# Fill matmuls, measured arrivals in the planner, and four low parts moved from GpSimd to VectorE in a fused attention, expert and MLP kernel

## The chip, the core and the metric

The kernel runs on one core of a Trainium2 chip. The metric is the device time of one execution in microseconds (us). Engines are named as the profile names them: PE is TensorE (matmuls; PEld is its weight load), DVE is VectorE, ACT is ScalarE, POOL is GpSimd, SP is SyncE, which issues most of the transfers.

## What is computed

Three stages follow each other, all in float32.

Attention: q, k, v of shape (4, 8, 576, 64); scores are q.k/8 plus a slope per head times the distance, kept for the 128 latest keys alone, then a softmax and the product with v. The result is 2304 rows of 512 numbers, x.

Experts: each row is normalised, multiplied by eight normalised expert vectors and divided by tau; the best expert is taken, and its softmax probability is the row's weight. The row of the output is `gate * (relu(x @ w1[e]) @ w2[e])`, with w1 of (8, 512, 1024) and w2 of (8, 1024, 512).

MLP: `h = x @ w_in` (512 to 2048), then 0 below -1, h above 1 and (h+1)^2/4 between, then `@ w_out`.

## The kernel before

Products of float32 accuracy are made from two parts of each operand: a high part, which is the operand rounded by a ScalarE copy (`whi`, `kh`, `hh`), and a low part, which is the operand less its high part (`wlo`, `kl`, `hl`), a subtraction on VectorE or GpSimd.

**Attention** is cut into 72 units: 8 groups `g` (a pair of batches and a pair of heads) by 9 tiles `t` of 128 queries. Tiles 0 to 3 take the first batch of the pair, 4 to 7 the second, and tile 8 the last 64 queries of both. A unit (`unit`, L802 on) goes through these steps: scores on PE (`sc`, L826 and L827; L822 for tile 8), mask and maximum on DVE (`ss`, `mx`, L839), exponential on ACT (`at`, L847), transposes on PE (`tp`, L854), their copy on DVE or ACT (`aT`, L859, L861), the product with the values on PE (`av`, L873), and in `finish` the division by the row sums (`rs`, L884, L886). Beside it run: the loads of q and k (`qk_loads`, 16 of them, the first in two cuts of columns, L608; then L621), their split into parts (`split_block`, L659 to L665; `split_rest`, L675 and L677, for tile 8), small products of the values with the expert vectors (`ven_steps`, `ep`, L690), and the routing of the rows.

**Routing** runs for the first half of the rows (pair 0) within attention, and for the second half at its end. `route` picks each row's expert and its slot, with a count on PE (`rp`, L361 to L365) and masks (`ocp`, `oap`) that PE turns into tables (`tabp`, L404). `roots(pr)` takes the root of the rows' squares in small steps over 128x9 numbers (`root`, L117 to L141), on POOL for pair 0 and on DVE for pair 1. `gates(pr)` makes the weights (L476 to L506) and a table of them (`tabg`, L519).

**Between attention and the expert loop** PE takes 128 rows of the first expert through that expert early and unsplit (`first_rows`: `hpe`, L1172; `hTe`, L1185; `ye`, L1197), while DVE ends the routing. The rest of the rows are gathered by POOL (L1119), scaled, transposed (`bx`) and split (`xh`, `xl`). In this time four chunks of the first expert's weights are split for the loop: `conv` asks for a high part on ACT (L536) and a low part on POOL (L541). After its low part, `convert_lo` issues the load of chunk i+6 on SP.

**The expert loop** (L1363 on) and the MLP follow, with PE busy nearly all the time.

**The order of the work** up to the expert loop comes from a planner that runs when the kernel is built. Every piece of work is a stream that yields an `ask`: an engine with a planned cost, an earliest time, events to wait for, a ring of buffers. `drive` picks the ask that can start first (ties by rank), issues its instruction and moves on, so each engine's order of instructions is the planned one; the chip then executes each engine's list in that order. An ask with `port=True` is planned so that DVE and POOL don't run such steps at the same time (`held`). `arrival` plans when a load lands. `warm_up` issues nine bf16 matmuls of 512 columns, and more until planned time 10.5, as long as nothing else is to be done on PE. The planned end of attention is `base`, and CONV gives for each of the four chunks the earliest high part and low part after it.

Of the kernel before, what the change touches and what calls it, by code (L numbers as in the profile page):

```python
# [8 lines left out]
F32 = mybir.dt.float32  # L9
# [10 lines left out]
P = 128  # L20
B, H, S, D = 4, 8, 576, 64
# [7 lines left out]
NP = B // 2  # L29
# [3 lines left out]
NRAW, NW, LEAD = 6, 7, 5  # L33
NEARLY = 5
BIAS = {"V": 1.2}
CONV = ((0, 0.0, 1.0), (1, 0.9, 1.5), (2, 3.0, 9.0), (3, 4.5, 11.0))
PEN = (0.03, 0.0, 0.8)
NWARM = 9
WARM = 10.5
TICK = 3.4133  # L40
EROOT = "V"
LATE = (0.4, 0.2, 0.5, 0.5, 0.2, 0.3)
# [9 lines left out]
C1 = D + 1 + E  # L52
# [7 lines left out]
def fused_kernel(ctx, tc, qk, vT, v, emb, tau, w1, w2, win64, wout64, out):  # L60
# [94 lines left out]
    streams, asks, rank_of = [], {}, {}  # L155
    busy = dict.fromkeys("PAVGS", 0.0)
    seen, rings, work, held = {}, {}, {}, {}
    now, end, on, at_unit = [0.0], [0.0], ["", None], [0.0]

    def ask(engines, start=0.0, after=(), ring=None, late=None, duty=None, port=False):  # L160

        return engines, start, after, ring, late, duty, port

    def add(stream, rank=0.0, ready=None):
        rank_of[stream] = rank
        asks[stream] = None, now[0] if ready is None else ready, (), None, 0.0, None, False
        streams.append(stream)
# [20 lines left out]
    def drive(more):  # L188
        while more():
            best = None  # L190
            for s in streams:
                c = first_start(s)
                if c and (best is None or c[:2] < best[0][:2]):
                    best = c, s
            (_, _, e, took, start), s = best
            ring = asks[s][3]
            if ring:
                rings[ring].remove(min(rings[ring]))
            if e == "P":

                k = int(start / TICK)
                work[k] = work.get(k, 0.0) + took * (asks[s][5] or 1.0)
                if work.get(k - 1, 0.0) < 0.375 * TICK:
                    took *= 2
            now[0], end[0], on[:] = max(now[0], start), start + took, [e, s]
            if e:
                busy[e] = end[0]
                if asks[s][6]:
                    held[e] = end[0]
            r = next(s, StopIteration)  # L210
            if r is StopIteration:
                streams.remove(s)
            elif r is None:
                asks[s] = vec()
            elif isinstance(r, tuple):
                asks[s] = r
            else:
                asks[s] = None, start + r, (), None, None, None, False
# [5 lines left out]
    dma = [0.0]  # L224

    def arrival(size):
        dma[0] = max(dma[0], end[0] + 0.65) + size / 0.36e6
        return dma[0] + 0.9

    rs_ = ExitStack()  # L230
    pr_ = rs_.enter_context(tc.tile_pool(name="pr", bufs=1, side="right"))
# [224 lines left out]
    def roots(pr):  # L456

        cols = slice(pr * NT, (pr + 1) * NT)
        yield ask({"V": 0.08}, after=of_tiles("squares", pr * NT, NT) + of_tiles("most squares", pr * NT, NT))
        nc.vector.tensor_tensor(nsq[:, cols], nsq[:, cols], nsq3[:, cols], op=ALU.add)  # L460
        e = "V" if pr == NP - 1 else "G"
        yield from root_steps(pr_, nrm[:, cols], nsq[:, cols], "p", e)
        seen["root", pr] = end[0] + 0.13

    def root_steps(pool_, out_, s_, nm, e):
        for n, _ in enumerate(root(pool_, out_, s_, nm, nc.vector if e == "V" else nc.gpsimd)):
            yield ask({"V": 0.08} if n < 2 or e == "V" else {"G": 0.19}, end[0] + 0.13, port=True)
# [94 lines left out]
    with ExitStack() as a:  # L562
# [38 lines left out]
        def qk_loads(n):  # L601
            g, b = divmod(n, 2)
            if n == 0:
                raw[0, 0] = new_raw()
                for c, cols in enumerate(CUT):
                    for x in range(2):
                        yield ask({"S": 0.45})
                        nc.sync.dma_start(raw[0, 0][:, x, :, cols], qk[0, 0, :, x, :, cols])  # L608
                        seen["qk"[x], 0, 0, c] = seen["qk"[x], 0, 1, c] = arrival(P * 8 * (cols.stop - cols.start))
                    if c == 0:  # L610
                        yield ask({"S": 0.45})
                        nc.sync.dma_start(embt, emb)
                        seen["emb"] = arrival(0)
            else:
                yield ask({"S": 0.45}, after=[("loads", n - 1)] + ([("split", n - 3)] if n >= 3 else []))
                raw[g, b] = new_raw()
                pr, hp = divmod(g, H // 2)
                for x in range(2):
                    if x:
                        yield ask({"S": 0.45})  # L620
                    nc.sync.dma_start(raw[g, b][:, x], qk[2 * pr + b, hp, :, x])  # L621
                    seen["qk"[x], n] = arrival(P * 8 * S)
            seen["loads", n] = now[0]
# [75 lines left out]

        CUT = (slice(0, 256), slice(256, S))  # L700
        lpt = pa.tile([P, NT, H, E], F32, name="lpt")

        def raw_experts():

# [57 lines left out]
        def warm_up():  # L762

            t = pa.tile([P, 1], BF16, name="warm")
            nc.vector.memset(t, 0.0)
            w = ps_av.tile([P, 512], F32, tag="av", name="warm_up")
            again = lambda: nc.tensor.matmul(w, t.to_broadcast([P, P]), t.to_broadcast([P, 512]), start=True, stop=True)
            for i in range(NWARM):
                again()
            busy["P"] = 0.87 + 0.427 * NWARM  # L770
            work.update({0: 0.5 * (TICK - 0.87), 1: 0.5 * (busy["P"] - TICK)})
            while True:
                yield ask({"P": 0.215}, late=LATE[5])
                if now[0] > WARM:
                    break
                again()
            rings["av"].append(end[0])

        def bias_of(h):
            yield ask({"V": 0.35}, 2.1)  # L780
# [21 lines left out]
        def unit(i):  # L802
# [61 lines left out]
            yield ask({"P": 0.449 * nb}, end[0] + 0.15, order("s3") + [("ven", g, x) for x in ((0, 1) if b is None else (b,))], None if n else "av", duty=0.57)  # L864
            seen["s3", u] = end[0]
            if n == 0:
                av_t[g] = ps_av.tile([P, 2, 2, C1], F32, tag="av", name="av")
            av = av_t[g]
            for j in range(2):
                for x, o in ((b, slice(0, P)),) if b is not None else ((0, slice(0, D)), (1, slice(D, P))):  # L870
# [60 lines left out]
            nc.gpsimd.memset(t, 0.0)  # L931
        nc.gpsimd.memset(one, 1.0)
        busy.update(A=0.7, V=0.5, P=0.5, S=0.63, G=3.0)
        rings.update(xp=[0.0] * 2, sc=[0.0] * 2, ss=[0.0] * 2, at=[0.0] * 4, tp=[0.0] * 2, aT=[0.0] * 3, av=[0.0])
        add(warm_up(), 1000.0)
        def load_tau():
            yield ask({"S": 0.45}, 5.0)
            nc.sync.dma_start(taut, tau.rearrange("(a b) -> a b", a=1).broadcast_to([E, 1]))
# [26 lines left out]
            add(gates(pr), rank + 5.0)  # L965
        add(early_rows(), 61.0)
        drive(lambda: len(finished) < len(units))


    pool = lambda st, name, bufs, **k: st.enter_context(tc.tile_pool(name=name, bufs=bufs, reuse_waits="tile", **k))  # L970
# [119 lines left out]
    with ExitStack() as bb:  # L1090
# [60 lines left out]
        def conv(i, t, j, u):  # L1151

            yield ask({"A": 0.95}, base + t, [("raw", i)])
            convert_hi(i, pw)
            yield ask({"G": 2.31}, max(end[0] + 0.13, base + u), [("lo", j - 1)] if j else [])
            convert_lo(i, nc.gpsimd, i + NRAW < 8)
            seen["lo", j] = end[0]
            if i + NRAW < 8:
                raws[i + NRAW] = wraw[i + NRAW]
                seen["raw", i + NRAW] = arrival(P * 4096)  # L1160
# [447 lines left out]
```

## Time and profile before

| | |
|---|---|
| median of 3 runs | 841.91 us (841.09 to 844.17) |
| the profiled execution | 842.7 us, span 841.0 us |
| busy share of the span | PE 97%, PEld 90%, DVE 63%, ACT 50%, POOL 17% |
| mean granted clock of PE | 0.979 of full speed |
| attention ends, first matmul of the expert loop | about 180 us, 204.01 us |

In the rows below, a timeline row has the start in us, the duration in us, engine, line, operation, output and input names with shapes and a count, and in brackets the idle time before it with what ended it. A row of the stretches has its limits, its length, and the busy time of PE, PEld, DVE, ACT and POOL with the instruction count of each; then the granted clock of PE (1.00 is 2.4 GHz, 0.50 is 1.2 GHz), the share of the DMA engines, and GB/s.

### The profile page before, as it was taken

Reading aid. Unit: us, or ns where it says so; the run is one execution under the profiler, and the core shown is the slowest. Engines: PE = TensorE matmul, PEld = TensorE weight load, DVE = VectorE, ACT = ScalarE, POOL = GpSimd, SP = SyncE. Lnnn points to the kernel's source line nnn. Section 1 sums busy time; section 2 is a strip of 40 time slices with the busy share of each in tenths; the row PEclk is TensorE's granted clock in tenths of the full one; section 3 lists DMA queues with packets and bytes.
Section 4 is the critical chain, followed back from the end, with each engine's and each line's share of the span. In section 5 each row is a group of like instructions: output and inputs, shape, how many; then the busy total and the mean of one; then the engine's idle time right before and its main releaser. Section 6 shows DMA issues by size and latency. Waiting matters only on the chain.

```text
span 841.0 us, 14144 instructions
## 1 busy us (share of the span) xinstructions
PE 816.4 (97%) x5195; PEld 757.7 (90%) x5195; DVE 529.9 (63%) x1390; ACT 419.4 (50%) x871; POOL 145.8 (17%) x206
## 2 busy tenths in 40 slices
PE   7999999879999999999999999999999999999996
PEld 5999898767999999999999989898999999999995
DVE  6676787599667767877639998644334445334332
ACT  5769888673553465667525555433222234223222
POOL 3756754226101001100000000003000003001001
PEclk7899999898999999999999999999999999999999
DMA  8566866035754486778323443022000012000000
GB/s 317 192 212 232 316 221 231 15 125 158 244 184 160 141 282 220 244 250 270 113 63 113 137 123 129 1 76 76 1 1 0 1 37 77 1 1 38 1 1 37
DMA packets 59690, 106.00 MB, mean 126 GB/s; under 512 B 3942, under 2 KB 36710, under 8 KB 59616
## 3 DMA queue, kind: packets, MB, share of 16 engines
q1 hardware_dynamic: 56288, 95.15, 34.4%
q0 software_dynamic: 3328, 9.90, 3.3%
q8 instruction: 41, 0.67, 0.3%
q14 instruction: 33, 0.27, 0.1%
HBM read 90.42 MB, written 14.62 MB: 125 GB/s over the span
## 4 chain that ended last, share of the span: by engine, by line
issue 55%; PE 11%; POOL 2%; DVE 1%; ACT 1%; DMA 0%; POOLq 0%; ACTq 0%
POOL out L1537 2%; PE bh L1411 2%; PE bh L1413 2%; PE bh L1412 2%; PE by L1400 2%; PE by L1402 2%; PE by L1401 2%; PE bx L1248 1%; DMA wraw<-in_w 0%; ACT whi L536 0%; DVE wlo L541 0%; POOL gap L1536 0%; POOL xg L1119 0%; PE permp L1338 0%; ACT yo L1450 0%
## 5 line engine op out<-in xcount | busy, mean ns | idle before, releaser
L1492 PE MATMUL ch<-yh,wc_0h 128*128 128x384 f32 x384 | 129.2, 336 | 0.0
L1494 PE MATMUL ch<-yh,wc_0l 128*128 128x384 f32 x384 | 129.1, 336 | 0.0
L1493 PE MATMUL ch<-yl,wc_0h 128*128 128x384 f32 x384 | 128.7, 335 | 0.0
L1500 DVE SCALAR_TENSOR_TENSOR r<-r 128x384 f32<-128x384 f32 x96 | 53.4, 556 | 119.4 <-ACT r L1498 119.3
L1498 ACT ACTIVATE r<-ch,halfc 128x384 f32<-128x384 f32 x96 | 55.2, 575 | 116.7 <-PE ch L1494 116.6
L1520 PE MATMUL o<-wc_1l,gh 128*128 128x512 f32 x288 | 113.3, 393 | 0.0
L1519 PE MATMUL o<-wc_1h,gl 128*128 128x512 f32 x288 | 113.1, 393 | 0.0
L1503 ACT ACTIVATE gh<-r 128x384 fp32r<-128x384 f32 x96 | 50.5, 526 | 123.6 <-DVE r L1502 123.6
L1518 PE MATMUL o<-wc_1h,gh 128*128 128x512 f32 x288 | 112.0, 389 | 0.0
L1537 POOL DMA_INDIRECT out<-ot,permu x18 | 17.5, 975 | 462.2 <-ACT ot L1532 459.3
L541 DVE TENSOR_TENSOR wlo<-wraw,whi 128x1024 fp32r<-128x1024 f32 x60 | 73.3, 1223 | 20.6 <-ACT whi L536 20.1
L1506 DVE TENSOR_TENSOR gl<-r,gh 128x384 fp32r<-128x384 f32 x96 | 53.4, 557 | 43.8 <-ACT gh L1503 43.8
L1411 PE MATMUL bh<-xh,whi 128*128 128x256 f32 (+6 forms) x256 | 80.3, 313 | 0.0
L1401 PE MATMUL by<-hl,whi 128*128 128x256 f32 (+6 forms) x256 | 77.3, 302 | 0.3 <-DVE hl L1417 0.2
L1400 PE MATMUL by<-hh,whi 128*128 128x256 f32 (+6 forms) x256 | 77.3, 302 | 0.0
L1402 PE MATMUL by<-hh,wlo 128*128 128x256 f32 (+6 forms) x256 | 77.3, 302 | 0.0
L1413 PE MATMUL bh<-xh,wlo 128*128 128x256 f32 (+6 forms) x256 | 77.1, 301 | 0.0
L1412 PE MATMUL bh<-xl,whi 128*128 128x256 f32 (+6 forms) x256 | 77.0, 301 | 0.0
L1492 PEld LDWEIGHTS ch<-yh,wc_0h 128*128 128x128 f32 x384 | 72.1, 188 | 2.9 <-DVE r L1502 0.3
L1493 PEld LDWEIGHTS ch<-yl,wc_0h 128*128 128x128 f32 x384 | 72.1, 188 | 2.5
L873 PE MATMUL av<-vt,aT 128*128 128x73 f32 (+1 forms) x576 | 67.4, 277 | 5.0 <-DVE rs L884 4.2
L1494 PEld LDWEIGHTS ch<-yh,wc_0l 128*128 128x128 f32 x384 | 72.0, 188 | 0.0
(271 smaller groups left out, 1759.5 us busy)
## 6 DMA issues: line engine op xcount, KB each, us to landing
wraw<-in_w SPq DMA_DIRECT2D x64, 512.0 KB, 4.1
rqk<-in_qk SPq DMA_DIRECT2D x30, 576.0 KB, 5.6
raw<-in_w_in SPq DMA_DIRECT2D x16, 512.0 KB, 4.1
raw<-in_w_out SPq DMA_DIRECT2D x16, 512.0 KB, 3.4
vT<-in_vT SPq DMA_DIRECT2D x16, 288.0 KB, 5.0
yl<-ysT SPq DMA_DIRECT2D x6, 768.0 KB, 4.8
x_dram<-xt SPq DMA_DIRECT2D x8, 512.0 KB, 3.7
vt<-in_v SPq DMA_DIRECT2D x8, 438.0 KB, 7.6
```

The source lines that it names most:

```text
L1400: nc.tensor.matmul(y, w2h[:, o], hh[:, :cap], start=(ff == 0), stop=False)
L1401: nc.tensor.matmul(y, w2h[:, o], hl[:, :cap], start=False, stop=False)
L1402: nc.tensor.matmul(y, w2l[:, o], hh[:, :cap], start=False, stop=(ff == 7))
L1411: nc.tensor.matmul(hp, w1h[:, o], xh[:, c, :cap], start=(c == 0), stop=False)
L1412: nc.tensor.matmul(hp, w1h[:, o], xl[:, c, :cap], start=False, stop=False)
L1413: nc.tensor.matmul(hp, w1l[:, o], xh[:, c, :cap], start=False, stop=(c == 3))
L1492: nc.tensor.matmul(hp, w1h[:, o], yh[:, c], start=(c == 0), stop=False)
L1493: nc.tensor.matmul(hp, w1h[:, o], yl[:, c], start=False, stop=False)
L1494: nc.tensor.matmul(hp, w1l[:, o], yh[:, c], start=False, stop=(c == 3))
L1518: nc.tensor.matmul(out_, gh[:, o], w2h, start=(ff == 0), stop=False)
L1519: nc.tensor.matmul(out_, gl[:, o], w2h, start=False, stop=False)
L1520: nc.tensor.matmul(out_, gh[:, o], w2l, start=False, stop=(ff == FF // P - 1))
```

## The change

Five things are altered. (1) The warm-up matmuls after the first nine are dropped; until attention is issued, `drive` puts matmuls of 220 columns before a PE step where the plan has PE idle and little work within the last TICK of planned time. They write the unused columns of the latest `av` tile, which is now 512 wide. (2) `arrival` counts 0.35 MB per us in place of 0.36 and 1.3 us of latency in place of 0.9; the load of the expert vectors goes behind all four loads of the first q and k. (3) The roots of pair 0 go to DVE as well. (4) The four low parts between attention and the expert loop go to DVE; the third and fourth wait for the weights of pair 1. (5) CONV asks for them earlier.

```diff
-CONV = ((0, 0.0, 1.0), (1, 0.9, 1.5), (2, 3.0, 9.0), (3, 4.5, 11.0))
+CONV = ((0, 0.0, 0.0), (1, 0.9, 1.5), (2, 3.0, 3.0), (3, 4.5, 4.5))
...
-WARM = 10.5
+FILL = 0.6
...
             if e == "P":
 
+                recent[:] = [x for x in recent if x[0] > start - TICK]
+                n = int(min(start - busy["P"], FILL * TICK - sum(x[1] for x in recent)) / 0.093) if warm else 0
+                for i in range(n):
+                    warm[0]()
+                    t = busy["P"] + 0.093 * (i + 1)
+                    recent.append((t, 0.093))
+                    work[int(t / TICK)] = work.get(int(t / TICK), 0.0) + 0.093
+
+                recent.append((start + took, took * (asks[s][5] or 1.0)))
...
     def arrival(size):
-        dma[0] = max(dma[0], end[0] + 0.65) + size / 0.36e6
-        return dma[0] + 0.9
+        dma[0] = max(dma[0], end[0] + 0.65) + size / 0.35e6
+        return dma[0] + 1.3
...
-        e = "V" if pr == NP - 1 else "G"
-        yield from root_steps(pr_, nrm[:, cols], nsq[:, cols], "p", e)
+        yield from root_steps(pr_, nrm[:, cols], nsq[:, cols], "p", "V")
...
-                    if c == 0:
-                        yield ask({"S": 0.45})
-                        nc.sync.dma_start(embt, emb)
-                        seen["emb"] = arrival(0)
+                yield ask({"S": 0.45})
+                nc.sync.dma_start(embt, emb)
+                seen["emb"] = arrival(1e5)
...
-            w = ps_av.tile([P, 512], F32, tag="av", name="warm_up")
-            again = lambda: nc.tensor.matmul(w, t.to_broadcast([P, P]), t.to_broadcast([P, 512]), start=True, stop=True)
+            latest[0] = ps_av.tile([P, 512], F32, tag="av", name="warm_up")
             for i in range(NWARM):
-                again()
+                nc.tensor.matmul(latest[0], t.to_broadcast([P, P]), t.to_broadcast([P, 512]), start=True, stop=True)
...
-            while True:
-                yield ask({"P": 0.215}, late=LATE[5])
-                if now[0] > WARM:
-                    break
-                again()
-            rings["av"].append(end[0])
+            recent.append((busy["P"], 0.5 * TICK))
+
+            def again():
+
+                n = latest[0][:, 4 * C1:]
+                nc.tensor.matmul(n, t.to_broadcast([P, P]), t.to_broadcast(list(n.shape)), start=True, stop=True)
+
+            return again
...
-                av_t[g] = ps_av.tile([P, 2, 2, C1], F32, tag="av", name="av")
+                latest[0] = ps_av.tile([P, 512], F32, tag="av", name="av")
+                av_t[g] = latest[0][:, :4 * C1].rearrange("p (t j c) -> p t j c", t=2, j=2)
...
-        rings.update(xp=[0.0] * 2, sc=[0.0] * 2, ss=[0.0] * 2, at=[0.0] * 4, tp=[0.0] * 2, aT=[0.0] * 3, av=[0.0])
-        add(warm_up(), 1000.0)
+        rings.update(xp=[0.0] * 2, sc=[0.0] * 2, ss=[0.0] * 2, at=[0.0] * 4, tp=[0.0] * 2, aT=[0.0] * 3, av=[0.0] * 2)
+        warm.append(warm_up())
...
         drive(lambda: len(finished) < len(units))
+        warm.clear()
...
-            yield ask({"G": 2.31}, max(end[0] + 0.13, base + u), [("lo", j - 1)] if j else [])
-            convert_lo(i, nc.gpsimd, i + NRAW < 8)
+            yield ask({"V": 1.15}, max(end[0] + 0.13, base + u), ([("lo", j - 1)] if j else []) + ([("gates", NP - 1)] if j > 1 else []), port=True)
+            convert_lo(i, nc.vector, i + NRAW < 8)
```

## Rows read from the trace of the kernel before

**Rows 1.** The page: the span, and the granted clock in 40 slices.

```profile
span 841.0 us, 14144 instructions
PEclk7899999898999999999999999999999999999999
```

**Rows 2.** The table by stretches.

```profile
30.00:140.00 110.00, 107.91 (x994) 104.18 (x993) 84.40 (x408) 94.29 (x241) 68.45 (x59) 1.00 0.68 236
...
6.00:11.00 5.00, 2.62 (x16) 1.92 (x15) 3.62 (x14) 2.05 (x7) 3.04 (x30) 0.99 1.02 358
...
11.00:27.60 16.60, 15.59 (x73) 15.22 (x73) 9.83 (x40) 9.85 (x23) 6.09 (x6) 0.50 0.90 336
...
139.00:142.00 3.00, 1.46 (x12) 1.25 (x11) 2.43 (x11) 1.55 (x6) 2.84 (x4) 1.00 1.05 384
...
152.40:157.70 5.30, 5.21 (x24) 5.25 (x25) 2.04 (x10) 2.11 (x7) 0.97 (x1) 0.50 0.02 3
189.00:195.20 6.20, 6.20 (x19) 3.57 (x19) 5.39 (x21) 0.54 (x2) 3.65 (x3) 0.50 0.26 78
```

**Rows 3.** The timeline of PE at the start.

```profile
5.07 0.82 PE L767 MATMUL warm_up<-warm 128*128 128x512 bf16 x3
...
8.21 0.38 PE L826 MATMUL sc<-kh,qs 128*128 128x256 f32 x1 [1.65 <-ACT kh L663]
...
29.74 0.36 PE L822 MATMUL sc<-kh,qz 128*128 128x256 f32 x1
```

**Rows 4.** The timelines of ACT, DVE and SP at the start.

```profile
6.93 0.31 ACT L675 ACTIVATE qz<-rqk 128x128 fp32r<-128x128 f32 x1 [1.26 <-DMA rqk<-in_qk]
...
11.50 0.61 ACT L659 ACTIVATE qs<-rqk 128x512 fp32r<-128x512 f32 x1
...
16.47 1.42 DVE L665 TENSOR_TENSOR kl<-rqk,kh 128x576 fp32r<-128x576 f32 x2
...
2.40 0.90 SPq L608 DMA_DIRECT2D rqk<-in_qk  x2
```

**Rows 5.** DVE and PE from 138 to 153 us, with POOL's group of low parts.

```profile
138.75 1.30 DVE L125 TENSOR_SCALAR rt_yp<-rt_ip 128x9 int32<-128x9 int32 x1
...
141.09 0.39 PE L826 MATMUL sc<-kh,qs 128*128 128x256 f32 x1 [1.54 <-DVE mx L839]
...
150.67 1.35 DVE L476 TENSOR_SCALAR inv<-nrm 128x9 f32<-128x9 f32 x1 [3.27 <-POOL nrm L141]
...
152.49 3.66 PE L873 MATMUL av<-vt,aT 128*128 128x73 f32 x16 [3.89 <-DVE rs L884]
...
L665 POOL TENSOR_TENSOR kl<-rqk,kh 128x576 fp32r<-128x576 f32 x4 | 5.7, 1426 | 0.2
```

**Rows 6.** POOL, DVE and PE between attention and the expert loop.

```profile
182.84 4.65 POOL L541 TENSOR_TENSOR wlo<-wraw,whi 128x1024 fp32r<-128x1024 f32 x2 [7.24 <-ACT whi L536]
...
182.96 2.26 DVE L132 TENSOR_TENSOR rt_tp<-rt_tp,rt_yp 128x9 f32<-128x9 f32 x1
...
185.25 2.27 DVE L135 SCALAR_TENSOR_TENSOR rt_yp<-rt_tp,rt_yp 128x9 f32<-128x9 f32 x1
...
189.35 0.16 DVE L135 SCALAR_TENSOR_TENSOR rt_yp<-rt_tp,rt_yp 128x9 f32<-128x9 f32 x1
...
193.00 2.97 DVE L500 CAST g<-gate_all 128x9 bf16<-128x9 f32 x1
...
207.71 2.35 DVE L541 TENSOR_TENSOR wlo<-wraw,whi 128x1024 fp32r<-128x1024 f32 x2
...
188.67 1.04 PE L404 MATMUL tabp<-oap,ocp 128*128 128x24 bf16 x10 [3.29 <-DVE oap L393]
...
204.01 0.69 PE L1411 MATMUL bh<-xh,whi 128*128 128x256 f32 x1
```

**Rows 7.** POOL's gathers before and beside low parts on DVE.

```profile
191.23 1.07 POOL L1119 DMA_INDIRECT xg<-x_dram,tabf  x1 [3.73 <-issue]
...
208.59 1.19 POOL L1119 DMA_INDIRECT xg<-x_dram,tabu  x1 [0.30 <-issue]
```

More of the change, by code (lines that the diff above doesn't have):

```diff
@@ L157, in fused_kernel @@
     seen, rings, work, held = {}, {}, {}, {}
+    recent, warm = [], []
     now, end, on, at_unit = [0.0], [0.0], ["", None], [0.0]
@@ L701, in fused_kernel @@
         lpt = pa.tile([P, NT, H, E], F32, name="lpt")
+        latest = [None]
         def raw_experts():
```

## The prediction

> **What bounds the kernel now.** I read the page first, then the table by stretches, then the timelines of the engines around each stretch where the clock row dips. TensorE works nearly everywhere, so the question is where it does not, or does so at half speed. The clock row has its low digits in three places: at the start, and in two of the slices near 150 and 190 us (each slice is 21 us) [rows 1]. The table by stretches gives them edges: the clock stands at 0.50, the lower of its two levels (1.2 instead of 2.4 GHz), from 11.0 to 27.6 us with 15.59 us of matmuls in it, from 152.4 to 157.7 with 5.21, and from 189.0 to 195.2 with 6.20 [rows 2]. Between 30 and 140 us TensorE is busy for 107.91 of 110 us at full clock, so attention as a whole hangs on TensorE [rows 2]. After 204 us the expert loop and what follows are dense too, and the change doesn't touch them: they only start earlier or later.
>
> Each of the three has an opening. At the start, TensorE does 2.62 us of work in 6 to 11 us, with one idle time of 1.65 us that ends with a ScalarE copy of the first keys [rows 2, 3]. That copy was late because ScalarE, in order, had sat 1.26 us at the remainder columns (L675) for a load of the second cut [rows 4]. At 148 us TensorE sits 3.89 us behind a VectorE instruction, which itself was behind 3.27 us of waiting for POOL's square roots [rows 5]. At 185 us TensorE sits 3.29 us for VectorE's routing masks; VectorE's two root instructions there took 2.26 and 2.27 us, where the same one takes 0.16 at 189.35, and POOL ran two low parts for 4.65 us just then [rows 6].
>
> **The start: fills and arrivals.** Removed are the three warm-up matmuls after the first nine [rows 3]; added are small bf16 matmuls of 220 columns wherever the plan sees TensorE idle and little work behind it. At best the whole half-clock stretch goes: 15.59/2 = 7.8 us. With arrivals 0.4 us later in the plan, ScalarE should no longer stand at L675 for the second cut ahead of the first cut's keys: 1.65 us. Upper end 7.8 + 1.65 = 9.4. What is late next is the second batch of q and k: ScalarE first touches it at 11.50, and VectorE ends its key lows at 16.47 + 1.42 = 17.9 [rows 4]. Four ScalarE steps of some 0.6 and a low part behind the last put the earliest end near 15.5 (an estimate from those rows), while TensorE, at full clock, is through the first batch near 13: 2.5 us of new wait. The trace shows no stretch in which half-filled time held the clock for as long as this, so I leave a quarter of 7.8, 1.9 us, for a fall of some length. 9.4 - 2.5 - 1.9 = **5.0 us**; lower end 0.5 (the better order alone, a third of the 1.65), upper end 9.4. The fills cost nothing where TensorE would wait, and if the plan's gap isn't there, each costs its columns: three of 512 took 0.82 us, so 220 are about 0.12. That the expert embedding's load now goes behind two loads on SP I count at nothing: its transposes lead to the small products of the values, which stand behind the first scores; without that cover it costs the issue of the two loads, 0.90 us [rows 4].
>
> **Roots of the first half on VectorE.** POOL loses its part of the chain (one step of -0.5, four in each of three rounds, the last product: 14) and VectorE gains 11 instructions (its fused form needs three a round). The wait of 3.27 us on VectorE goes, and with it TensorE's 3.89; the half-clock stretch behind it, 5.21/2 = 2.6, goes as well. Upper end 3.89 + 2.6 = 6.5. The 11 instructions at 0.16 are 1.8 us of VectorE beside its other work. But POOL makes the low parts of keys there, 1.43 us each, and a VectorE instruction with two SBUF inputs that meets one stands until it ends: a root step of 138.75 took 1.30, and TensorE then sat 1.54 [rows 5]. Now eleven can meet them. The plan keeps the two apart by its port rule, with times that the chip doesn't keep exactly, so I charge 1.4 such events of 1.43: 2.0 us. **4.5 us**; upper end 6.5, lower end -1 (half of the eleven blocked, 5.5 x 1.35 = 7.4, all passed on).
>
> **The low parts between attention and the experts.** POOL's four (2.3 us each) become four on VectorE, 2.35 us a pair [rows 6]. Two blocks of 2.26 + 2.27 - 2 x 0.16 = 4.2 us leave the routing chain, and two early lows come into it, as they become startable in the chain's small gaps: 2.35. So the masks come 1.85 us earlier and the wait of 3.29 becomes 1.4. An idle time of 1.54 us left the clock at 1.00 in 139 to 142 us [rows 2, 5], so the fall at 189 should not come: 6.20/2 = 3.1. Together 4.95. The third block, 2.97 on a cast of the router's weights, goes too [rows 6], so these come 1.85 + 2.8 = 4.65 us earlier, about as much as TensorE, and don't become late. Lows three and four now stand on VectorE behind the weights, 2.35 us ahead of the splits that the first expert's matmul at 204.01 needs; I take off 0.95 for that. **4.0 us**; upper end 3.29 + 3.1 = 6.4, lower end 0.5. SP issues the load of chunk 6 behind the first low, so it comes about 1 us earlier; chunks 8 and 9 wait for lows three and four, which end earlier than POOL's did.
>
> One thing speaks against lows on VectorE: POOL's gathers run beside them. A gather's issue took 1.07 us without a low beside it and 1.19 inside a pair of VectorE's lows [rows 7]: 0.12, nothing. The Trainium skill (SBUF — State Buffer, Who interferes with whom) warns that a DMA issued by GpSimd can starve while a VectorE instruction holds their shared port pair, though it infers that a tensor_tensor does not hold the half that descriptors need. By the warning the sum would be 12.3 instead of 13.5; the row above does not bear it out.
>
> **Sum.** 5.0 + 4.5 + 4.0 = 13.5. The profiled execution took 842.7 (span 841.0 and 1.7 around it), 0.8 above the median of the runs, 841.91. 842.7 - 13.5 = 829.2, so **829 us**, or 828.4 counted from the median.
>
> **Rivals.** A is the forecast: chance 0.48, own range 825 to 834.
> B, the clock falls at the start in spite of the fills: then the first term is 1.0, and the time 833. For it: the clock fell at 11 us after 2.62 us of work in five, and came back only at 27.6 though TensorE was busy for 15.59 of 16.6 us [rows 2]: TensorE's own work at the start holds it badly, and the fills must make up for that. Against: it was still 0.99 in 6 to 11 us, behind the warm-up [rows 2]. 0.18.
> C, roots blocked: half of the eleven meet POOL's lows, and the second term is -1: 835. For it: the 1.30 and 1.35 of rows 5. Against: the plan's port rule. 0.12.
> D, the early lows cost what they free: they stand between the count and the masks, VectorE is 2.35 us late there, the wait stays near 3 us and the clock falls again; third term 0.5: 833. It decides if the wait stays above some 2.5 us. 0.10.
> E, gathers held: the first gather waits for one low, 2.35/2 = 1.2 us [rows 6], and the first expert's rows are late by that: 830.4. 0.05, as the 0.12 us above speaks against it.
> F, the other side: fills in front of real work. They are allowed until attention ends, and from 30 to 140 us TensorE has only 2.1 us of idle time to hide them [rows 2]. If the plan sees gaps there that the chip doesn't have, each fill adds 0.12. It turns to slower by 0.5% from 13.5 + 4.2 = 17.7 us, some 150 fills; at 200 of them 842.7 - 13.5 + 24 = 853. Against: the plan would need 14 us of gaps where the chip shows 2.1. 0.07.
>
> **How the numbers follow.** About 0.5% (4.2 us) is what a measurement of this kernel can tell from no change. A, B, D and E lie below 837.7 alone, C mostly; two of B, C and D together (842.7 - 1.0 + 1.0 - 4.0 = 838.7 for B and C) do not, and make 0.12 for no change. Faster 0.80, same 0.12, slower 0.08. The range goes from 821, near all three upper ends (842.7 - 22.3 = 820.4), to 838, where two rivals meet; F and a little of the ends are left out.
>
> **What would show it.** Right: clock 1.00 through 11 to 27 us, the ninth unit's first score, now at 29.74 [rows 3], near 25; no wait of VectorE for POOL near 148 and no clock below 1.00 there; a wait at the masks under 2 us, the first expert matmul 13 us earlier than 204.01. Wrong: 0.50 in the first 30 us (B), VectorE root steps of over 1 us (C), a wait of 3 us at the masks (D), more than 100 fills in the dense stretch (F).

## The result, and the profile after

The changed kernel took 834.28 us (median of 4 executions, 831.67 to 837.68), the kernel before 842.79 beside it: a ratio of 0.988, with a 95% interval of 0.984 to 0.993. The forecast of 829 (821 to 838) had the direction right and the gain too large: 8.5 us where 13.5 were summed. The time lies in the stated range, just above the forecast's own, 825 to 834. The profiled execution took 836.59, its span is 834.9 (841.0 before), so its rows have to account for 6.1 us.

The page: span and granted clock in 40 slices.

```profile
span 834.9 us, 14146 instructions
...
PEclk6999999899999999999999999999999999999998
```

Set beside [rows 1], the low digit in the slice near 190 us is gone, the one near 150 is still there, and the first slice is lower than before. The table by stretches, in the columns of [rows 2]:

```profile
6.00:11.00 5.00, 3.16 (x17) 3.16 (x17) 3.92 (x15) 3.16 (x11) 3.05 (x30) 0.68 1.01 384
11.00:27.60 16.60, 16.60 (x89) 16.20 (x89) 11.68 (x46) 10.80 (x25) 5.84 (x5) 0.58 0.91 349
...
60.00:65.00 5.00, 5.00 (x25) 5.00 (x25) 2.06 (x12) 3.23 (x9) 2.23 (x3) 0.50 0.98 367
...
150.00:155.00 5.00, 4.24 (x22) 4.25 (x23) 2.65 (x17) 1.89 (x7) 0.14 (x1) 0.61 0.01 3
...
180.00:196.00 16.00, 15.67 (x99) 10.61 (x98) 14.81 (x64) 9.06 (x21) 4.04 (x4) 1.00 0.48 148
```

Two of the three dips of [rows 2] remain, and there is a new one: from about 59 to 66 us the clock is at its lower level, with TensorE busy for 5.00 of 5.00 us. The one between attention and the experts is gone: from 180 us to the first expert matmul TensorE is busy for 15.67 of 16.00 us at full clock, where before it was idle for 3.29 [rows 6].

PE's timeline, at the places that the prediction named:

```profile
4.66 0.45 PE L785 MATMUL warm_up<-warm 128*128 128x220 bf16 x3
...
7.84 0.56 PE L717 MATMUL etp<-ident,xt 8*128 8x8 f32 x4 [2.73 <-DMA xt<-in_emb]
8.33 0.58 PE L836 MATMUL sc<-kh,qs 128*128 128x256 f32 x1
...
28.64 0.36 PE L832 MATMUL sc<-kh,qz 128*128 128x256 f32 x1
...
150.76 3.37 PE L884 MATMUL av<-vt,aT 128*128 128x73 f32 x16 [1.19 <-DVE xt L913]
...
177.30 0.45 PE L785 MATMUL av<-warm 128*128 128x220 bf16 x3 [1.27 <-DVE rs L895]
...
196.18 0.68 PE L1423 MATMUL bh<-xh,whi 128*128 128x256 f32 x1
201.69 0.39 PE L1413 MATMUL by<-hl,whi 128*128 128x256 f32 x1 [1.53 <-DVE hl L1429]
```

There are six fills in all, three before the first scores and three at 177 us. TensorE then waits 2.73 us for the load of the expert vectors, with the first scores behind it. The ninth unit's score comes at 28.64 (29.74 in [rows 3]). The wait of 3.89 us near 148 [rows 5] has become 1.19. The first expert matmul comes 7.8 us earlier than in [rows 6], and a new wait of 1.53 us stands at the first product of `hl`.

DVE and POOL in the same execution:

```profile
139.95 1.02 DVE L125 TENSOR_SCALAR rt_yp<-rt_ip 128x9 int32<-128x9 int32 x1
...
148.92 1.25 DVE L485 TENSOR_SCALAR inv<-nrm 128x9 f32<-128x9 f32 x1
...
189.67 0.18 DVE L509 CAST g<-gate_all 128x9 bf16<-128x9 f32 x1
...
201.22 0.42 DVE L1429 SCALAR_TENSOR_TENSOR hl<-bh,hh 128x256 fp32r<-128x256 f32 x1
...
148.73 1.42 POOL L673 TENSOR_TENSOR kl<-rqk,kh 128x576 fp32r<-128x576 f32 x1 [1.17 <-ACT kh L671]
```

The cast that took 2.97 in [rows 6] takes 0.18. The first instruction of the gates (L485; L476 before) ends no earlier than POOL's low part of keys beside it, as in [rows 5].

**A way to read all runs.** Four rows cut any trace of this kernel into three: the start of the last 64-row product of attention, the first expert matmul, the first product of `hl`, and the end of the span. For the profiled execution of each kernel (us):

| kernel | last `av` starts | to first `bh` | to first `hl` product | from there to the end |
|---|---|---|---|---|
| before | 178.92 | 25.09 | 3.84 | 633.15 |
| the change | 177.87 | 18.31 | 5.51 | 633.21 |
| e1, lows alone | 189.61 | 18.57 | 5.56 | 633.96 |
| e2, roots alone | 176.70 | 25.62 | 3.82 | 633.36 |
| e3, start alone | 175.05 | 27.10 | 3.82 | 633.13 |
| e4, the change again | 175.01 | 18.33 | 5.52 | 633.34 |
| e5, more fills | 171.09 | 18.33 | 5.52 | 633.96 |
| e6, without the roots | 175.66 | 18.72 | 5.54 | 633.68 |
| e7, `starts` in the loop | 176.73 | 18.32 | 3.81 | 633.24 |
| e8, expert vectors early | 180.05 | 19.11 | 5.51 | 633.63 |
| e9, e7 again | 178.43 | 18.33 | 3.82 | 633.72 |
| e10, fills at the start | 179.75 | 18.33 | 3.82 | 633.50 |
| e11, fills at 59 us | 178.18 | 18.33 | 3.82 | 634.17 |
| e12, both fills | 173.97 | 18.33 | 3.81 | 633.29 |

The time to the first `bh` is 18.31 to 19.11 us in the eleven kernels with the low parts on VectorE (18.31 to 18.33 in eight of them) and 25.09 to 27.10 in the three with them on POOL; in e3, which has the 27.10, the clock is at 0.50 from 175 to 178 us as well. The next column takes two values, 3.81 to 3.84 and 5.51 to 5.56, and the last lies between 633.1 and 634.2. Only attention's end moves much from execution to execution (177.87 and 175.01 for the same code; 189.61 in e1, whose profiled execution is its longest, 849.37 where the median is 838.82). So the middle columns can be compared in single traces; attention needs many executions.

### The profile page after: what moved, and what is told of

It reads as the page before. It is cut to its first block, busy times and chain, and to the rows that moved or that the text cites. A ratio compares the mean times of both kernels' runs of the same rounds, so it can differ in the third digit from the quotient of the medians.

```text
span 834.9 us, 14146 instructions
## 1 busy us (share of the span) xinstructions
PE 815.1 (98%) x5198; PEld 759.3 (91%) x5198; DVE 529.0 (63%) x1405; ACT 421.2 (50%) x880; POOL 133.9 (16%) x188
## 4 chain that ended last, share of the span: by engine, by line
issue 56%; PE 12%; POOL 2%; ACT 0%; DVE 0%; POOLq 0%; ACTq 0%
PE bh L1423 2%; POOL out L1549 2%; PE bh L1425 2%; PE bh L1424 2%; PE by L1412 2%; PE by L1414 2%; PE by L1413 2%; PE bx L1260 1%; ACT whi L545 0%; DVE wlo L550 0%; POOL gap L1548 0%; PE permp L1350 0%; POOL xg L1131 0%; ACT yo L1462 0%; DVE cva L1026 0%
## 5 line engine op out<-in xcount | busy, mean ns | idle before, releaser
L550 DVE TENSOR_TENSOR wlo<-wraw,whi 128x1024 fp32r<-128x1024 f32 x64 | 78.1, 1222 | 20.6 <-ACT whi L545 19.6
```

## The experiments

Executions of the kernel before went along each time: medians of 844.23 (e1 to e4), 845.53 (e5 to e8) and 843.88 (e9 to e12). Lows, roots and start are parts 4 and 5, part 3, and parts 1 and 2. A gain in us below is what the ratio makes of the median of the kernel before; the difference of the two medians differs from it by up to 1 us (5.4, 5.6, 4.3 and 11.9 us for e1 to e4).

**e1, the lows alone.** The kernel before with these lines of the change:

```diff
-CONV = ((0, 0.0, 1.0), (1, 0.9, 1.5), (2, 3.0, 9.0), (3, 4.5, 11.0))
+CONV = ((0, 0.0, 0.0), (1, 0.9, 1.5), (2, 3.0, 3.0), (3, 4.5, 4.5))
...
-            yield ask({"G": 2.31}, ...
-            convert_lo(i, nc.gpsimd, i + NRAW < 8)
+            yield ask({"V": 1.15}, ...
+            convert_lo(i, nc.vector, i + NRAW < 8)
```

> The kernel before with the low parts and CONV of the change alone (parts 4 and 5); attention's order is that of before. Theory now, from the two profiles: nearly all of the gain is here. In the changed kernel the first expert matmul stands 18.3 us behind the last product of attention (196.18 after 177.87), in the kernel before 25.1 (204.01 after 178.92): 6.8 us, of which a new wait of 1.5 us at the first hl is given back. So 5.3 us faster, about 837. Rival, by the prediction's sum: 4.0 us, the clock's fall at 189 gone but lows three and four late for the splits.

Measured: 838.82 (12 executions), ratio 0.9947 (0.992 to 0.9973), 4.5 us. In the table the two middle columns fall from 28.93 to 24.13, 4.8 us: the ratio and the trace agree.

**e2, the roots alone.** `root_steps` for pair 0 on VectorE in the kernel before, nothing else.

```diff
-        e = "V" if pr == NP - 1 else "G"
-        yield from root_steps(pr_, nrm[:, cols], nsq[:, cols], "p", e)
+        yield from root_steps(pr_, nrm[:, cols], nsq[:, cols], "p", "V")
```

> The kernel before with the roots of the first half on VectorE alone (part 3). Prediction: 4.5 us faster (6.5 if no root step meets POOL's low parts). Theory now: about 2 us faster, as the wait of 3.89 us goes, but root steps and the first step of the gates still stand behind POOL's low parts of 1.4 us, TensorE still sits over 1 us once or twice near 150 us, and the clock falls there as before (0.50 for 7 us).

Measured: 838.67 (6), ratio 0.9928 (0.9903 to 0.9953), 6.1 us; the last three columns of the table stay as they were within 0.6 us, so it comes from attention. PE's timeline of this kernel has the two waits of [rows 5] in other sizes:

```profile
140.11 0.39 PE L825 MATMUL sc<-kh,qs 128*128 128x256 f32 x1 [2.95 <-DVE mx L838]
...
150.97 3.16 PE L872 MATMUL av<-vt,aT 128*128 128x73 f32 x16 [0.95 <-DVE xt L901]
```

The later one lost 2.9 us and the earlier gained 1.4, since root steps on VectorE now meet POOL's low parts there. Of the eleven steps that moved, four are held, for 0.80 to 1.27 us where one takes 0.16. Two of them in VectorE's timeline:

```profile
144.19 1.27 DVE L135 SCALAR_TENSOR_TENSOR rt_yp<-rt_tp,rt_yp 128x9 f32<-128x9 f32 x1
...
148.99 1.26 DVE L132 TENSOR_TENSOR rt_tp<-rt_tp,rt_yp 128x9 f32<-128x9 f32 x1
```

**e3, the start alone.** The change with parts 3 to 5 undone.

```diff
 (the change)
-        yield from root_steps(pr_, nrm[:, cols], nsq[:, cols], "p", "V")
+        e = "V" if pr == NP - 1 else "G"
+        yield from root_steps(pr_, nrm[:, cols], nsq[:, cols], "p", e)
...
-            convert_lo(i, nc.vector, i + NRAW < 8)
+            convert_lo(i, nc.gpsimd, i + NRAW < 8)
```

> The changed kernel with parts 3, 4 and 5 undone: fills, later arrivals and the expert vectors' load behind all four first loads. Prediction: 5.0 us faster, the clock kept through the first 28 us. Theory now: 0 to 1.5 us faster in most executions, as the plan puts only three fills ahead of a wait of 2.7 us for the expert vectors, and the clock falls at about 8 us; executions in which the clock doesn't fall there are faster by up to 5 us.

Measured: 839.9 (12), ratio 0.9959 (0.9932 to 0.9987), 3.5 us. The surprise is where they come from. The half-clock stretch at the start is there, but the wait near 148 is not, though the roots are on POOL as before:

```profile
141.92 0.39 PE L837 MATMUL sc<-kh,qs 128*128 128x256 f32 x1 [1.24 <-DVE mx L850]
144.15 0.39 PE L837 MATMUL sc<-kh,qs 128*128 128x256 f32 x1 [0.38 <-DVE mx L850]
155.28 0.78 PE L885 MATMUL av<-vt,aT 128*64 128x73 f32 x16 [1.68 <-ACT aT L872]
```

With the new arrivals the plan orders this place otherwise, and VectorE waits 0.75 us for POOL's roots in place of 3.27:

```profile
150.62 1.37 DVE L486 TENSOR_SCALAR inv<-nrm 128x9 f32<-128x9 f32 x1 [0.75 <-POOL nrm L141]
```

Parts 1 and 2 remove most of the very wait that part 3 was meant for.

**e4, the change again**, on the chip of e1 to e3.

> The changed kernel as it is, for its executions' clocks beside their times. Theory now: two levels, near 836 with a mean granted clock of 0.979 (0.50 for 17 us at the start) and near 831 with 0.986 or more (the start kept at full clock). Rival: the times don't follow the clock, and the spread of 6 us is between chips or runs.

Measured: 832.34 (6), ratio 0.9869 (0.9844 to 0.9894), 11.1 us, where the three parts alone gave 4.5 + 6.1 + 3.5 = 14.1. By these numbers the parts overlap by some 3 us. Each of the four has an interval of some 2 us either way, so the numbers alone don't show the overlap; the wait that e3 already removes does.

**e5, more fills.** Twenty more fills ahead of the first scores, with the order of the work kept.

```diff
+                for i in range(int((start - busy["P"]) / 0.093) - n if warm and start < 14.0 else 0):
+                    warm[0]()
```

> The change with 20 more fills: each planned gap of TensorE before planned time 14 is filled whole, in the same order of the work (23 fills ahead of the first scores in place of 3). Theory now: the clock stays at or near full for longer in the first 28 us, and the time is at most 1.5 us better than the change (ratio to before 0.985 to 0.987), since the second batch of q and k and the in-order waits bound the start. Rival, the first term of the prediction: half of the 17 us at half clock comes back, 4 to 5 us, ratio 0.981 to 0.982.

Measured: 835.57 (6), ratio 0.9874 (0.9818 to 0.9931), no better than the change. The clock stayed up to 12.5 us and then fell:

```profile
10.00:12.00 2.00, 1.72 (x10) 1.08 (x10) 1.54 (x12) 1.71 (x5) 0.12 (x4) 1.00 1.01 397
12.00:14.00 2.00, 1.13 (x6) 0.89 (x6) 1.63 (x3) 2.00 (x5) 0.00 (x0) 0.63 1.04 423
14.00:16.00 2.00, 2.00 (x12) 2.00 (x11) 1.97 (x3) 0.44 (x2) 0.47 (x1) 0.50 1.02 412
```

At full clock TensorE runs out of work here (busy for 1.13 of 2.00 us), and the ninth unit's score comes at 27.61, 1.2 us earlier than in e4 (28.78).

**e6, the change without the roots** (the lines of e2, undone in the change).

> The change with part 3 undone: the roots of the first half stay on POOL. Theory now: the two parts remove the same wait (with the new arrivals alone the 3.89 us near 148 us is gone from the profile), so the roots are worth 1 to 3 us on top of the others: ratio to before 0.989 to 0.991 where the change has 0.987. Rival: the parts add, the roots are worth their 6 us here too: ratio 0.994.

Measured: 836.03 (6), ratio 0.9881 (0.9826 to 0.9936). Against the change's 0.9869 and 0.9882 the roots on VectorE seem to be worth about 1 us or less on top of the rest, where alone they were worth 6.1; the intervals, 4.6 us either way here, are too wide to put a figure on it.

**e7, `starts` in the loop.** In the change, VectorE runs the steps of `starts` (offsets of the experts, needed only later) between the last splits and the first `hl`. This kernel spreads them over the first expert's rounds.

```diff
-            for _ in starts():
-                yield vec(0.15, late=LATE[4])
+            next(later)
...
+                if e == 0 and ff >= 1:
+                    for _ in range(2):
+                        next(later, None)
```

> The change with the small steps of starts() behind erank_i (14 VectorE instructions) moved into the first expert's loop, two a round, so that they no longer stand ahead of the first hl. Theory now: the wait of 1.53 us at the first hl goes, the ratio to before falls by 0.0018, to about 0.985. Rival: the next low part or the load of chunk 8 is late in its place, and nothing is gained.

Measured: 831.76 (6), ratio 0.9822 (0.9766 to 0.9878). PE's timeline:

```profile
195.05 0.69 PE L1423 MATMUL bh<-xh,whi 128*128 128x256 f32 x1
...
198.86 0.28 PE L1413 MATMUL by<-hl,whi 128*128 128x256 f32 x1
```

The wait is gone: 3.81 us from the first `bh` to the first product of `hl`, where the change has 5.51, and nothing is given back behind it (633.24 in the table's last column, 633.21 in the change).

**e8, the expert vectors early.** Their load goes back behind the first two loads, as before the change.

```diff
-                yield ask({"S": 0.45})
-                nc.sync.dma_start(embt, emb)
-                seen["emb"] = arrival(1e5)
+                    if c == 0:
+                        yield ask({"S": 0.45})
+                        nc.sync.dma_start(embt, emb)
+                        seen["emb"] = arrival(1e5)
```

> The change with the expert vectors' load back between the first and second cut of q and k. Theory now: the wait of 2.7 us ahead of the first scores goes and they start near 6 us in place of 8.3; little of it is left at the ninth unit, whose first score comes at 28 us or later, since the second batch bounds it: at most 1.5 us better than the change. Rival: the whole 2.5 us stay, ratio 0.984.

Measured: 835.05 (6), ratio 0.9868 (0.9808 to 0.9929). The first scores come at 6.40 in place of 8.09 to 8.33, but the ninth unit's only at 28.16, where the change has 28.64 and e4 28.78. So most of the 2.73 us that TensorE waits for this load is not missed at 28 us. This kernel differs in more than the load, though: its plan puts 17 fills into the first 18 us, and its clock in the first 30 us is 0.83, not 0.72.

**e9 to e12: e7 again, and fills where they hold the clock.** e9 is e7's kernel, as the base of the three others. e10 adds three fills ahead of every step of TensorE planned between 9 and 20 us (57), e11 four ahead of each pair of small products planned between 50 and 64 us (24), e12 both.

```diff
+                for i in range(3 if warm and 9.0 < busy["P"] < 20.0 else 0):
+                    warm[0]()
...
+                for i in range(4 if warm and asks[s][5] in (0.1, 0.13) and 50.0 < busy["P"] < 64.0 else 0):
+                    warm[0]()
```

> The kernel of the run with starts() in the first expert's loop, again, as the base of the three that follow. Theory (the 1.5 us at the first hl are the only thing that this edit takes away): 1.5 us under the change's 832 to 834, so 830.5 to 833, no wait at the first product of hl, clock at 0.50 for about 17 us at the start and some 6.8 us behind the run of small products at 58 us. Rival (that gain was luck of the executions): 833 to 836.

> On top of the base: three fills ahead of every step of TensorE that the plan puts between 9 and 20 us, 57 in all, some 57 x 0.1 = 5.7 us of TensorE at full clock, where the change has 16 us of half-speed work. Theory (at the start the second batch's data sets the time, the clock hardly matters): the clock stays at 1.00 through 11 to 25 us, but the ninth unit's first score comes no earlier than 27, against 28.7, and the median is within 2 us of the base, better or worse. Rival (the clock is what costs, as the prediction's first term had it): the ninth unit near 25, the median 3 to 4 us under the base, 827 to 829. Third outcome: the fills don't hold the clock either, 0.50 stays and the ninth unit comes 3 or more us later: 834 to 838.

> On top of the base: four fills ahead of each pair of small products of the values that the plan puts between 50 and 64 us, 24 in all, 24 x 0.1 = 2.4 us. Theory (the long run of products of 16 columns lets the clock fall at 59 us, though TensorE has no idle time): no half clock in 58 to 67 us, 6.83/2 = 3.4 us back for 2.4 us of fills, so 1 us faster than the base in the executions where the clock fell there, slower by 2.4 in those where it didn't; median within 1.5 us of the base. Rival (the fall has to do with something else that the records don't show): the half clock in 58 to 67 stays and the run is 2.4 us slower than the base.

> Both sets of fills on top of the base, to see if a kernel with a whole clock through attention is fastest. Theory (data at the start, products at 59): within 2 us of the base, granted clock of the execution 0.99 or more, 829 to 834. Rival (the clock is what costs at both places): 826 to 828.

Measured, six executions each: e9 835.29 (0.9876, 0.9843 to 0.991), e10 833.68 (0.988, 0.9852 to 0.9907), e11 835.49 (0.9887, 0.9861 to 0.9913), e12 835.05 (0.9894, 0.9871 to 0.9917). e9 has the wait at `hl` removed as in e7, yet its median is 3.5 us above e7's and 2.9 above e4's: attention's own scatter is larger than the 1.7 us, and no version is shown to beat the change.

In e12 the clock is at 0.50 from 8.4 to 11.8 us, and full from there to 141 us, where it falls once more. Its table by stretches, and the ninth unit in PE's timeline:

```profile
12.00:18.00 6.00, 5.69 (x56) 5.54 (x56) 5.03 (x13) 3.87 (x9) 0.58 (x1) 1.00 1.03 416
18.00:28.00 10.00, 9.86 (x93) 9.60 (x93) 7.39 (x32) 6.98 (x17) 5.64 (x5) 1.00 0.78 286
...
140.00:150.00 10.00, 8.66 (x63) 8.67 (x63) 9.00 (x45) 8.23 (x21) 7.37 (x8) 0.83 0.44 164
```

```profile
28.25 0.36 PE L834 MATMUL sc<-kh,qz 128*128 128x256 f32 x1
```

So with the clock at 1.00 where the change had 0.50, the ninth unit is 0.5 us earlier than in e4. That does not say that the clock is worth nothing here, since the fills took time too. e10 has the same 57 fills, and the same list of TensorE instructions up to the ninth unit; in its profiled execution the clock stayed at 0.50 until 17.8 us in spite of them, and the ninth unit comes at 30.75:

```profile
30.75 0.36 PE L834 MATMUL sc<-kh,qz 128*128 128x256 f32 x1
```

So between these two the clock goes with 2.5 us, and with the fills and the half clock of e10 the ninth unit is 2.0 us later than in e4. The theory's clock of 1.00 from 11 us on failed in that execution, which is close to the third outcome. In the medians the theory holds for both kernels (within 2 us of the base), and the ninth unit comes no earlier than 27; the rival's 827 to 829 for e10 and 826 to 828 for e12 did not come.

e11 settles the new dip at 59 us as far as one profile can. The change and e11, PE's timeline at the 14 small products, then e11's stretch:

```profile
58.49 2.55 PE L698 MATMUL ep<-xt,vT 128*128 128x16 f32 x14
```

```profile
59.41 0.53 PE L700 MATMUL ep<-xt,vT 128*128 128x16 f32 x4
59.78 0.55 PE L787 MATMUL av<-warm 128*128 128x220 bf16 x4
```

```profile
60.00:65.00 5.00, 4.94 (x46) 4.74 (x44) 2.79 (x18) 3.76 (x10) 2.79 (x3) 1.00 0.90 326
```

With fills between them the clock held. But e5 has the same 14 products in one piece, and there it held too:

```profile
57.45 1.63 PE L700 MATMUL ep<-xt,vT 128*128 128x16 f32 x14
```

Eight traces have this run in one piece (one of the 14 records is missing in e10). The dip stands in five (the change, e3, e4, e7, e9) and not in three (e5, e6, e10). In the kernel before, with the products split up by others, it doesn't stand. So the fall goes with the run, but the run doesn't force it; what decides is open. The fills did not pay for themselves in the median (835.49 to 835.29).

## Why the prediction was right in direction and too large

**The start, 5.0 us summed.** This is the term that failed most: its clock was not held, and its profiled gain is 1.1 us. Two statements in it failed. "At best the whole half-clock stretch goes": the clock was lost at 8 us, earlier than before, and came back at about 25. The plan allowed three fills here, since it counts half of the warm-up as recent work; the prediction took the fills as if every idle time got them. "That the expert embedding's load now goes behind two loads on SP I count at nothing": its transposes (`etp`) stand ahead of the first scores on TensorE, and did so in the kernel before, where they came in time:

```profile
4.75 0.38 PE L708 MATMUL etp<-ident,xt 8*128 8x8 f32 x4
...
5.72 0.38 PE L826 MATMUL sc<-kh,qs 128*128 128x256 f32 x1
```

With the load behind, the first scores came at 8.33 in place of 5.72. Rival B, given 0.18, named the outcome and nearly its size: 1.0, and 29.74 became 28.64, 1.1 us. That its total of 833 is near the measured 834 is partly luck: the start alone gave 3.5 us in e3, by another wait, and the other two terms were off as well.

The price of the clock, 15.59/2 = 7.8 us, was worked out in the order of work of the kernel before, and in that order the traces bear most of it out. The change brought another order, in which the same clock seems to be worth much less. The kernel before, e2 and e1 have the same list of TensorE instructions up to the ninth unit's first score, and so have e4, e6 and e5 but for e5's 20 fills, which lie ahead of the first scores. Each row is a single execution:

| order | profiled execution of | mean granted clock, 0 to 30 us | ninth unit's first score |
|---|---|---|---|
| of before | before | 0.72 | 29.74 |
| | e2 | 0.77 | 27.29 |
| | e1 | 0.89 | 25.12 |
| of the change | e4 | 0.72 | 28.78 |
| | e6 | 0.77 | 27.96 |
| | e5 | 0.83 | 27.61 |

The stretch of [rows 2] in e1, where the clock is at 0.50 only until 15.2 us, and its ninth unit:

```profile
11.00:27.60 16.60, 15.46 (x119) 15.19 (x119) 13.97 (x55) 13.12 (x30) 7.33 (x10) 0.87 0.95 360
```

```profile
25.12 0.36 PE L822 MATMUL sc<-kh,qz 128*128 128x256 f32 x1
```

In the old order (0.89 - 0.72) x 2 x 30 = 10 us less of half clock go with 4.6 us, nearly their half, and with the "near 25" that the prediction asked for. In the new order (0.83 - 0.72) x 2 x 30 = 6.6 us less go with 1.2. One place where the clock is hidden there can be read: at 13.1 us TensorE waits for the same ScalarE copy in e4, at half clock, and in e5, at full clock until 12.5 us.

```profile
13.12 1.13 PE L884 MATMUL av<-vt,aT 128*128 128x73 f32 x4 [0.33 <-ACT aT L871]
```

```profile
13.14 1.13 PE L886 MATMUL av<-vt,aT 128*128 128x73 f32 x4 [0.87 <-ACT aT L873]
```

Executions without a trace point the same way for the new order. Each carries its granted clock, and a mean of c leaves about (1 - c) x 2 x 830 us for half clock (in the traces it is 1.5 to 5 us less): 5 us at 0.997, too little for the 17 us of the start; 20 at 0.988; 33 at 0.980. Pairs of executions of one kernel at the higher two levels: the change 831.96 at 0.995 and 831.67 at 0.986, e9 830.06 at 0.997 and 829.49 at 0.988, e7 829.2 at 0.997 and 829.8 at 0.988, e4 830.85 at 0.998 and 832.78 at 0.985, e3 838.6 at 0.995 and 838.01 at 0.987. The mean difference is 0.2 us. (e11 is not among them: 835.84 at 0.996, 832.81 at 0.997, 831.3 at 0.987.) That it is the start's stretch which is missing at 0.997 is inferred, as no execution with that clock has a trace. What holds the new order all the way to 28 us is open: the loads (DMA share 1.01 to 1.04 from 10 to 16 us in e5) are a candidate, but no run took them away.

Later in attention, where TensorE is dense, half clock costs its full half. From the ninth unit to the last `av` the kernel before takes 149.2 us and e1 164.5, with 6.8 and 37.5 us at half clock in them (counted in steps of 1 us); less half of these it is 145.8 and 145.7. The executions agree: from 0.988 to 0.980, e9 goes from 829.49 to between 835.22 and 836.21, and the change from 831.67 at 0.986 to 836.59 and 837.68 at 0.979, 5 to 6.7 us for some 13 us of half clock.

**The roots, 4.5 us summed.** Alone they gave 6.1, within the bounds of -1 and 6.5. What failed is that the terms were added. The 3.89 us were booked here, but the new order of parts 1 and 2 removes most of them by itself (e3). Rival C (half of the eleven blocked) did not come: in the two traces of the change none of the eleven takes more than 0.72 us, where in e2, in the old order, four were. Two blocks remained, L125 at 1.02 and L485 at 1.25. Neither is among the eleven; both ran on VectorE before, and were held there too (1.30 and 1.35 in [rows 5]). So the 3.89 us held a part, behind the 1.35 of L476, that moving the roots could not remove, and TensorE's 1.19 is what is left of it. The prediction spoke of instructions with two SBUF inputs, but L125 and L485 have one. The Trainium skill (SBUF — State Buffer, Who interferes with whom) names tensor_scalar and cast among the operations that can take the port pair shared with GpSimd, and these rows agree (1.25 and 1.02 where the same forms take 0.16 to 0.17 alone). TensorE's 1.19 is followed by the clock at 0.61. In e12 the same instruction met no low part (0.17 us) and 150 to 160 us ran at full clock; in e4 the wait was there, 1.18, and the clock stayed up. So a wait of this size is not enough by itself.

**Between attention and the experts, 4.0 us summed.** This term was too small in one place and missed another. From the last product of attention to the first expert matmul the change saves 25.09 - 18.31 = 6.8 us. The masks stood 1.9 us closer behind the last product (`tabp` at 185.74 - 177.87 = 7.87 us, before 188.67 - 178.92 = 9.75), as the prediction's 1.85 had it. But the wait did not shrink to 1.4, it vanished: in the new order TensorE has the early rows' matmuls to do while VectorE works, and is busy for 15.67 of 16 us. Nothing came back for lows three and four, for which 0.95 were taken off. Then 5.51 - 3.84 = 1.7 us go again at the first `hl`: eighteen small steps of `starts` and its neighbours stand ahead of it on VectorE, from 198.12 us on in the change. They stood there before too, but with 3.84 us to the first product TensorE did not have to wait for them; now it arrives 6.8 us earlier. That is "what is late next", and the prediction looked for it at the splits alone. Net 5.1 in the trace, 4.5 by e1's ratio. Rival D did not come.

Of E the mechanism came, and not the cost. The change's VectorE and POOL:

```profile
193.79 2.35 DVE L550 TENSOR_TENSOR wlo<-wraw,whi 128x1024 fp32r<-128x1024 f32 x2
...
194.99 1.97 POOL L1131 DMA_INDIRECT xg<-x_dram,tabu  x1 [0.30 <-PE bx L1260]
```

This gather began just behind the start of the second low, which ended at 196.14, and ended 0.82 us after it; it took 1.97 where the seven other gathers up to 202 us take 0.95 to 1.10. The same gather takes 1.96 or 1.97 in all eleven kernels with the lows on VectorE. The 1.19 of [rows 7], from which the prediction read "0.12, nothing", fits too: that gather began 0.34 us before its low ended, and ended 0.85 us after it, so the small number was luck of the moment. The Trainium skill (SBUF — State Buffer, Who interferes with whom) infers that a tensor_tensor leaves room for descriptors. These rows show a gather held beside one all the same; which part of its work was held is open. TensorE didn't wait for this gather, so the hold of 1 us cost nothing here.

**F, fills in front of real work**, did not come: six fills in all.

**The sum.** By e4's ratio 11.1 us: 5.1 of them between attention and the experts, some 6 within attention. How the 6 divide is not shown. There the waits near 140 and 148 became shorter, and executions with little half clock more frequent: 6 of the change's 10 lie at 0.985 or above, against 1 of the 45 of the kernel before shown with e1 to e12. The profiled execution of the change has two stretches of half clock behind the start's (59 and 151 us), so it shows only 1.05 us of that: 1.05 + 6.8 - 1.7 = 6.15 of its 6.1.

## What to carry to other kernels

Before pricing a stretch at half clock, ask what the work behind it waits for, and ask it in the order that the change brings: the same stretch cost nearly half of its length in the old order here and about a fifth of it in the new one. Fills that hold the clock take time as well. Terms that end at the same wait can't be added; when a change also reorders a plan, treat every wait near an edit as one that the new order may already have removed. And when a consumer is made earlier by several microseconds, look through the whole list of the engine that feeds it, up to its first product, not only at the wait that is being removed.

## What the hardware did that was not expected

The same kernel's executions differ in granted clock from 0.979 to 0.998 for the change and from 0.967 to 0.990 for the kernel before, and with it in time by 7 and by 14 us; behind attention their profiled executions repeat to within 0.2 us where the code is the same (the change and e4). The clock fell at 59 us with TensorE busy all the time, in a run of small products, and stayed up in the same run of three other traces. And a single 1.2 us wait at 150 us was followed by half clock in the change, e9, e10 (2.21 us there) and e11, but not in e4. A gather that POOL issued beside a low part on VectorE was held to that low's end: 1.97 us in place of 0.95 to 1.10.
